# The MLP's second product of an adaLN block, by output features instead of by tokens

## The chip, the cores and the metric

The kernel runs on one core of one Trainium2 chip. The metric is the device time of the program in microseconds (us): the median of 3 runs before is 785.61 us (784.95 to 787.28). TensorE (PE) multiplies, VectorE (DVE) and ScalarE (ACT) work on vectors, GpSimd (POOL) does small things and issues some transfers, and SyncE (SP) issues most of the transfers. Matmul results go to PSUM, which the kernel uses as eight banks of 128 partitions x 512 numbers of 4 bytes.

## The reference

One transformer block, 2048 tokens of 640 features, with a modulation that is drawn from a single vector c. The second half is what matters here:

```python
mod = (_silu(c) @ w_mod).reshape(c.shape[0], 6, 1, -1)
sa, ca, ga, sb, cb, gb = (mod[:, i] for i in range(6))
h = _layernorm(x, axis=-1) * (1 + ca) + sa
x = x + ga * _A_ref(h, A_wqkv, A_w_phi, A_wo)      # linear attention, 32 heads of 20
h = _layernorm(x, axis=-1) * (1 + cb) + sb
# _B_ref: F = 1728
h = jnp.einsum("bsd,df->bsf", h, w1) + b1
r = jnp.where(h > 0, h, 0)
h = r * r
out = jnp.einsum("bsf,fd->bsd", h, w2) + b2
x = x + gb * out
```

## The kernel before

Every large product is computed in three terms: each operand is split into a rounded high half and the rest (`three`: high x high, high x low, low x high). ScalarE makes the high half by a copy into the rounded type, VectorE the low half by a subtraction (`lo`, line 80, so all of them show as L80). `mm` (line 70) issues the matmuls, so all of them show as L70; the tiles' names tell them apart.

**Stages.** First the projections and the state of the attention (to about 265 us), then the attention's output for the first 1024 tokens, then the MLP in four groups `g` of 512 tokens (`GW`): groups 0 and 1, then `attend` (attention's output for the last 1024 tokens, pairs of token tiles `j` = 4 to 7), then groups 2 and 3. In the last two stages the order of PE, DVE and ACT is written out by hand (`manual_schedule`): the program order of the Python code is the order on each of these engines. SP and POOL are ordered by a planner. The first 265 us are mostly ordered by that planner too.

**One group.** The hidden layer is cut into 14 chunks `f` of 128 features (the last has 64). Step f of `group` issues the first product of chunk f (`up_mm`: 15 matmuls of 512 columns, weights standing, tokens moving), its ReLU, square and split (`up_relu`, `up_out`), and the second product of chunk f - 2 (`down`, LAG = 2). `down` has the tokens stand (128 x 128 of the squared hidden layer, tile r2t) and the weights w move, 640 columns in cuts of 384 and 256: 4 token tiles x 2 cuts x 3 terms = 24 matmuls a chunk, 16 in the last. The sums stay in PSUM for the whole group: four banks of tag pj (tile acc) and two of tag m (tile acr). `up_mm` is left with one bank of tag tp (odd f) and the third of tag m (even f).

**The end of a group.** For each token tile `finish` multiplies the sums by the gate gb (`gb_b`, spread over all partitions) and adds the residual, to which `add_b2` added b2 x gb before. `residual` loads the residual x1 as four tiles of 128 tokens, one store per tile writes the output. In the last group the gate is multiplied into W2 instead (`round2`: multiply on DVE, high half on ACT, low half on DVE).

**Weights.** W1 stays for the most part; four chunks of W1 and all of W2 go through a ring of six slots, loaded some chunks ahead (`ring_loads`). For W2 the raw chunk is read and rounded again (`round2`, L1477), the low half is read from a copy in DRAM.

**Around attention.** `late_blocks`/`late_turn` load and turn blocks of the attention's features (32 x 32 transposes on DVE, L948), `num` multiplies them with the state on PE, `num_hi` and `num_lo` split the result on ACT and DVE, `do_wo` multiplies with wo and adds the residual. `ln2`, `back`, `turn`, `affine`, `split2` make the next groups' inputs H2. Buffers are rows of tags s1 to s4, x, k, q0, q1 and w (`BUFS`); an instruction that writes a new tile waits until the slot's last user is done.

## Time and profile before

| | us |
|---|---|
| median of 3 runs | 785.61 (784.95 to 787.28) |
| the profiled execution | 786.04 |
| its span | 784.3 |
| first matmul of group 0, from the span's start | 348.0 |
| group 1's first up matmul | 445.2 |
| attention for the last 1024 tokens, its first matmul | 535.5 |
| group 2's first matmul | 589.1 |
| last matmul | 779.8 |

The granted clock of TensorE is 0.999 over the span. Busy shares over the span: PE 99%, DVE 71%, ACT 51%, POOL 10%. By stage, VectorE is busy 68.8 of the 97 us from 348 to 445, 76.9 of the 91 us to 536, 43.3 of the 61 us to 597, 37.1 of the 87 us to 684, and 54.6 of the last 100 us; the DMA engines' share in the same stages is 0.84, 0.78, 0.69, 0.58 and 0.31.

How to read the rows: times are us from the span's start. A row of a group of instructions has line, engine, operation, out<-in, shape of the output (partitions x elements), count, then busy time in us, mean ns of one, then the idle time of the engine before them and who ended it. A timeline row has start, length, engine, line, operation, shape, count, and in brackets the wait before it. A row of the windows has the stretch, its length, then busy time (and count) of PE, its weight loads, DVE, ACT and POOL, the granted clock, the share of the DMA engines and GB/s. Rows of transfers have KB of one and the median us from issue to landing; rows of one tile give min/median/max in ns.

### The profile page before, as it was taken

Reading aid. Unit: us, or ns where it says so; the run is one execution under the profiler, and the core shown is the slowest. Engines: PE = TensorE matmul, PEld = TensorE weight load, DVE = VectorE, ACT = ScalarE, POOL = GpSimd, SP = SyncE. Lnnn points to the kernel's source line nnn. Section 1 sums busy time; section 2 is a strip of 40 time slices with the busy share of each in tenths; the row PEclk is TensorE's granted clock in tenths of the full one; section 3 lists DMA queues with packets and bytes.
Section 4 is the critical chain, followed back from the end, with each engine's and each line's share of the span. In section 5 each row is a group of like instructions: output and inputs, shape, how many; then the busy total and the mean of one; then the engine's idle time right before and its main releaser. Section 6 shows DMA issues by size and latency. Waiting matters only on the chain.

```text
span 784.3 us, 13311 instructions
## 1 busy us (share of the span) xinstructions
PE 775.4 (99%) x5163; PEld 716.2 (91%) x5163; DVE 553.4 (71%) x917; ACT 402.7 (51%) x789; POOL 78.8 (10%) x181
## 2 busy tenths in 40 slices
PE   9999999999999999999999999999999999999997
PEld 8899999999998988898999989998999999989997
DVE  4499899999766488664869799957945353575544
ACT  4667576546744344655957355432365544433221
POOL 3002020001100022201323000100010000000000
PEclk9999999999999999999999999999999999999999
DMA  9613248234121254476799757996679855145121
GB/s 339 259 36 132 101 164 290 91 129 153 55 85 34 84 191 137 163 223 234 254 313 336 236 182 250 262 364 189 189 238 353 280 162 158 51 151 201 34 84 68
DMA packets 76437, 142.31 MB, mean 181 GB/s; under 512 B 12718, under 2 KB 37422, under 8 KB 76374
## 3 DMA queue, kind: packets, MB, share of 16 engines
q1 hardware_dynamic: 69094, 117.41, 45.7%
q0 software_dynamic: 4096, 16.78, 5.7%
q10 hardware_dynamic: 3184, 7.27, 2.6%
q8 instruction: 40, 0.66, 0.3%
q14 instruction: 23, 0.19, 0.1%
HBM read 98.40 MB, written 42.93 MB: 180 GB/s over the span
## 4 chain that ended last, share of the span: by engine, by line
PE 82%; DVE 7%; DMA 4%; ACT 3%; POOL 2%; issue 1%; SPq 0%; ACTq 0%; DVEq 0%; POOLq 0%
PE up L70 22%; PE acc L70 14%; PE acr L70 9%; PE pv L70 9%; PE pk L70 9%; PE pq L70 8%; PE pwo L70 4%; PE kvp L416 3%; DVE dn L814 2%; DVE scr L812 1%; DMA rw<-in_w 1%; PE ta L326 1%; DVE ezb L833 1%; DMA xb<-in_x 1%; DMA w<-w2d 1%
## 5 line engine op out<-in xcount | busy, mean ns | idle before, releaser
L70 PE MATMUL up<-h,w 128*128 128x512 f32 (+1 forms) x910 | 198.2, 371 | 1.1 <-ACT r L1375 0.8
L70 PEld LDWEIGHTS up<-h,w 128*128 128x128 f32 x910 | 155.8, 188 | 29.1 <-DVE h L80 1.2
L70 PE MATMUL acc<-w,r2t 128*128 128x384 f32 x656 | 150.8, 336 | 0.0
L70 PE MATMUL acr<-w,r2t 128*128 128x256 f32 x656 | 112.9, 279 | 0.0
L70 PEld LDWEIGHTS acc<-w,r2t 128*128 128x128 f32 x656 | 107.5, 188 | 4.2 <-DVE w L80 0.2
L70 PEld LDWEIGHTS acr<-w,r2t 128*128 128x128 f32 x656 | 105.6, 188 | 0.0
L70 PE MATMUL pwo<-wo,ot 128*128 128x320 f32 (+1 forms) x512 | 79.5, 313 | 0.1
L70 PE MATMUL pk<-wk,hT 128*128 128x320 f32 x480 | 79.1, 313 | 0.1
L70 PE MATMUL pv<-wv,hT 128*128 128x360 f32 (+1 forms) x480 | 78.3, 312 | 0.0
L70 PE MATMUL pq<-wq,hT 128*128 128x320 f32 x480 | 76.7, 314 | 0.5 <-ACT k L392 0.4
L70 PEld LDWEIGHTS pwo<-wo,ot 128*128 128x128 f32 (+1 forms) x512 | 75.8, 188 | 1.1 <-DVE xm L1044 0.4
L70 PEld LDWEIGHTS pk<-wk,hT 128*128 128x128 f32 x480 | 71.5, 188 | 2.5 <-issue 0.9
L70 PEld LDWEIGHTS pv<-wv,hT 128*128 128x128 f32 x480 | 72.4, 188 | 0.4
L70 PEld LDWEIGHTS pq<-wq,hT 128*128 128x128 f32 x480 | 70.6, 188 | 2.1 <-ACT k L392 1.3
L1375 ACT ACTIVATE r<-up,b_t 128x512 f32<-128x512 f32 x52 | 35.0, 680 | 67.6 <-PE up L70 59.6
L80 DVE TENSOR_TENSOR r2t<-r,r2t 128x512 fp32r<-128x512 f32 (+1 forms) x56 | 38.3, 685 | 32.9 <-ACT r2t L1387 30.1
L1386 DVE TENSOR_TENSOR r<-r 128x512 f32<-128x512 f32 x26 | 17.9, 690 | 47.0 <-ACT r L1375 47.0
L80 DVE TENSOR_TENSOR w<-rw,w 128x640 fp32r<-128x640 f32 (+2 forms) x42 | 33.3, 814 | 23.6 <-ACT w L1074 12.1
L1387 ACT ACTIVATE r2t<-r 128x512 fp32r<-128x512 f32 x52 | 32.9, 632 | 22.4 <-DVE r L1386 21.6
L1477 ACT ACTIVATE w<-rw 128x640 fp32r<-128x640 f32 x42 | 30.6, 730 | 26.4 <-DVE rw L1476 24.1
L339 ACT ACTIVATE hfa<-ta,cols_a 128x256 f32<-128x256 f32 x30 | 17.0, 565 | 27.0 <-PE ta L326 25.8
L1074 ACT ACTIVATE w<-rw 128x640 fp32r<-128x640 f32 x28 | 19.4, 727 | 16.6 <-DMA rw<-in_w 7.5
(241 smaller groups left out, 1078.9 us busy)
## 6 DMA issues: line engine op xcount, KB each, us to landing
rw<-in_w SPq DMA_DIRECT2D x65, 320.0 KB, 4.5
w<-w2d SPq DMA_DIRECT2D x28, 320.0 KB, 6.0
w<-w1d SPq DMA_DIRECT2D x12, 640.0 KB, 6.6
esp<-eq SPq DMA_DIRECT2D x11, 640.0 KB, 3.2
wm<-in_w_mod SPq DMA_DIRECT2D x20, 320.0 KB, 3.6
xb<-in_x SPq DMA_DIRECT2D x8, 640.0 KB, 4.4
el<-esp SPq DMA_DIRECT2D x8, 640.0 KB, 4.0
xx<-in_x SPq DMA_DIRECT2D x16, 320.0 KB, 3.7
```

Of the source, the lines that this page charges most:

```text
L70: nc.tensor.matmul(o, a, b, start=first and i == 0, stop=last and i == len(terms) - 1, skip_group_check=skip,)
L80: (eng or nc.vector).tensor_tensor(out_lo, full, hi.bitcast(F32), op=ALU.subtract)
L326: nc.tensor.transpose(p[:, i * P : (i + 1) * P], xn[:, i, d * P : (d + 1) * P], ident)
L339: nc.scalar.activation(hf, p[:, :256], AF.Identity, bias=cols[:, d : d + 1], scale=cols[:, 5 + d : 6 + d])
L416: nc.tensor.matmul(kvp[64 * c : 64 * c + 64, g // 4, a : a + 2 * n].rearrange("p (s n) -> p s n", s=2), v[:, u], e[:, :, o : o + n], start ...
L812: nc.vector.tensor_tensor(z, flat(ET[t]), flat(zb), op=ALU.mult)
L814: nc.vector.tensor_reduce(dn.rearrange("p s h -> p (s h)"), heads(z), axis=AX.X, op=ALU.add)
L1074: nc.scalar.activation(w[:, 0], RAW[k, f], AF.Copy)
L1375: nc.scalar.activation(r, UP[f], AF.Relu, bias=b1_t[:, f : f + 1])
L1386: nc.vector.tensor_tensor(r, r, r, op=ALU.mult)
L1387: nc.scalar.activation(t[:, 0], r, AF.Copy)
L1477: nc.scalar.activation(w[:, 0], raw, AF.Copy)
```

## The change

The second product is turned round. The weights of chunk f stand, 128 of the 640 output features at a time (five output chunks k), and all 512 tokens move: 15 matmuls of 512 columns a chunk, 10 for the last. The sums are then features x tokens, in five banks (four pj, one m), and `up_mm` has three banks in rotation. Since an output feature is now a partition, gate and b2 x gate are columns of one number per partition: ScalarE applies both while it evicts (`gated`, scale and bias). VectorE transposes the result in 32 x 32 blocks and adds the residual, which is loaded in the layout that these blocks have (`residual`, `finish`), and the output is stored from there in rows of 640 bytes (`store`). The output features are permuted in the weights w2, b2 and part 5 of w_mod, as before in parts 3 and 4.

The order at the ends of groups changes with it. After groups 0 and 2, three chunks are evicted and finished at the group's end, chunks 3 and 4 in steps 0 and 1 of the next group. After group 1 all five are evicted between the last matmuls, three are finished there and two in `attend` at j = 5, and the store follows there. The turning of block 5 moves from group 1's end into its steps 12 and 13. In the last group the first product of the last chunk is put ahead, the second products of chunks 10 to 13 run output chunk by output chunk, the last two output chunks in halves of 256 tokens; W2 isn't multiplied by the gate any more, and its low half is read as in the other groups. The stores of x1 for j = 4, 5 are issued on ACT, xx5 has another buffer, and tag s3 has five rows instead of three.

```diff
-BUFS = {"w": 21, "x": 2, "k": 2, "q0": 1, "q1": 1, "s1": 3, "s2": 2, "s3": 3, "s4": 5}
+BUFS = {"w": 21, "x": 2, "k": 2, "q0": 1, "q1": 1, "s1": 3, "s2": 2, "s3": 5, "s4": 5}
...
-    gb_b = const.tile([P, D], F32, name="gb_b")
-    bb = const.tile([P, D], F32, name="bb")
+    gate = const.tile([P, NC], F32, name="gate")
+    b2g = const.tile([P, NC], F32, name="b2g")
...
-    X1 = [dram.tile([P, 2, D], F32, name=f"x1_{j}") for j in range(NT // 2)]
+    X1 = [dram.tile([2 * P, D], F32, name=f"x1_{j}") for j in range(NT // 2)]
...
-        yield from mod_rows(5, gb_b)
-        t = row("s1", "b2s")
-        nc.sync.dma_start(t, bass.AP(tensor=b2.tensor, offset=b2.offset, ap=[[0, P], [1, D]]))
-        nc.vector.tensor_tensor(bb, t, gb_b, op=ALU.mult)
+        yield from mod_cols(5, gate)
+        nc.sync.dma_start(b2g, b2)
...
-                nc.sync.dma_start(X1[j], XM[j])
+                (nc.sync if j < FIRST else nc.scalar).dma_start(X1[j].rearrange("(i p) d -> p i d", p=P), XM[j])
...
-            XX[j] = [row("s4" if j == 5 else "s2" if j < 4 else "s1", f"xx{j}_{i}") for i in range(2)]
+            XX[j] = [row("s2" if j < 6 else "s1", f"xx{j}_{i}") for i in range(2)]
...
-    def behind_sp():
-        return tc.issue_after([i for i in nc.cur_bb.bb.instructions if i.engine == ET_.SP][-1])
+    def behind(engine):
+        return tc.issue_after([i for i in nc.cur_bb.bb.instructions if i.engine == engine][-1])
...
-            UP[f] = tp(f"up{g}_{f}") if f % 2 and f != extra else bank(f"up{g}_{f}")
+            UP[f] = tp(f"up{g}_{f}") if f % 3 == 1 else bank(f"up{g}_{f}")
...
-    ACC, XR = {}, {}
-    CUT = 384
-
-    def residual(g):
-        with behind_sp():
-            for i in range(4):
-                t = XR[g, i] = row("s4", f"xr2_{g}_{i}")
-                nc.sync.dma_start(t, X1[2 * g + i // 2][:, i % 2])
-
-    def add_b2(g):
-        for i in range(4):
-            nc.vector.tensor_tensor(XR[g, i], XR[g, i], bb, op=ALU.add)
-
-    def down(g, f, tiles=range(4)):
+    ACC, XR, YT = {}, {}, {}
+
+    def residual(g, r):
+        if r == 0:
+            XR[g] = []
+        rows = g + 1 < NGR
+        t = row("s4", f"xr{g}_{r}") if rows else flat(tok2("x", f"xr{g}_{r}"))
+        XR[g].append(t)
+        n = P if rows else 2 * P
+        j, at = divmod(n * r, 2 * P)
+        src = X1[2 * g + j][at : at + n].rearrange("(b i) f -> i b f", i=32)
+        with behind(ET_.PE):
+            for a in range(4):
+                nc.sync.dma_start(t[32 * a : 32 * a + 32].rearrange("p (b f) -> p b f", f=160), src[:, :, 160 * a : 160 * a + 160])
+
+    def down(g, f, ks=range(NC), cols=None):
         t, n, w = R2[g, f], FS[f], W2[f]
-        for i in tiles:
-            if f == 0:
-                if i == 0:
-                    big = pj(f"acc{g}_0") + pj(f"acc{g}_1")
-                    rest = [bank(f"acr{g}_{h}") for h in range(2)]
-                    for h in range(4):
-                        ACC[h] = (big[h][:, :CUT], rest[h % 2][:, 256 * (h // 2) : 256 * (h // 2) + 256])
-            s = slice(i * P, (i + 1) * P)
-            for h, cs_ in enumerate((slice(0, CUT), slice(CUT, D))):
-                if n == P:
-                    terms = three(t[:, 0, s], t[:, 1, s], w[:, 0, cs_], w[:, 1, cs_])
-                else:
-                    terms = [(t[:, 0, s], w[:, 0, cs_]), (t[:, 0, s], w[:, 1, cs_])]
-                mm(ACC[i][h], terms, first=(f == 0 and (h == 0 or i < 2)), last=(f == NF - 1), skip=(h == 1))
-
-    def finish(g, i):
-        y, more = XR[g, i], g + 1 < NGR
-        z = row("s3", f"z{g}_{i}") if more else None
-        for h, cs_ in enumerate((slice(0, CUT), slice(CUT, D))):
-            src = ACC[i][h]
-            if more:
-                nc.vector.tensor_tensor(z[:, cs_], src, gb_b[:, cs_], op=ALU.mult)
-                src = z[:, cs_]
-            nc.vector.tensor_tensor(y[:, cs_], src, y[:, cs_], op=ALU.add)
-        t = 4 * g + i
-        nc.sync.dma_start(out[t * P : (t + 1) * P], y)
+        c = cols or slice(0, GW)
+        for k in ks:
+            if f == 0 and k == 0:
+                ACC.update(enumerate(pj(f"acc{g}_0") + pj(f"acc{g}_1") + [bank(f"acc{g}_4")]))
+            hi, low = (w[:, s, k * P : (k + 1) * P] for s in range(2))
+            terms = [(hi, t[:, 0, c]), (hi, t[:, 1, c]), (low, t[:, 0, c])] if n == P else [(hi, t[:, 0, c]), (low, t[:, 0, c])]
+            mm(ACC[k][:, c], terms, first=(f == 0), last=(f == NF - 1), skip=(g == NGR - 1 and k > 2))
+
+    def gated(g, k, cols=slice(0, GW)):
+        if cols.start == 0:
+            YT[k] = row("s3", f"yt{g}_{k}")
+        nc.scalar.activation(YT[k][:, cols], ACC[k][:, cols], AF.Identity, bias=b2g[:, k : k + 1], scale=gate[:, k : k + 1])
+
+    def finish(g, k, cols=slice(0, GW)):
+        n = GW // len(XR[g])
+        y = row("s3", f"y{g}_{k}")
+        nc.vector.transpose(*(t[:, cols].rearrange("p (b e) -> p b e", e=32) for t in (y, YT[k])))
+        for r in range(cols.start // n, cols.stop // n):
+            to = XR[g][r].rearrange("p (b f) -> p b f", f=160)[:, :, 32 * k : 32 * k + 32]
+            nc.vector.tensor_tensor(to, y[:, n * r : n * r + n].rearrange("p (b e) -> p b e", e=32), to, op=ALU.add)
+            if k == NC - 1 and g + 1 != FIRST // 2:
+                store(g, r, n)
+
+    def store(g, r, n):
+        at = GW * g + n * r
+        dst = out[at : at + n].rearrange("(b i) f -> i b f", i=32)
+        src = XR[g][r].rearrange("p (b f) -> p b f", f=160)
+        for a in range(4):
+            q = nc.scalar if a % 2 and r and g + 1 == NGR else nc.sync
+            q.dma_start(dst[:, :, 160 * a : 160 * a + 160], src[32 * a : 32 * a + 32])
...
-                if gg < NGR - 1:
-                    nc.sync.dma_start(w[:, 1].bitcast(F32), WD[k][i])
+                nc.sync.dma_start(w[:, 1].bitcast(F32), WD[k][i])
...
-    def round2(g, f):
+    def round2(f):
         if 0 <= f < NF:
-            n, w, raw = FS[f], W2[f], RAW[f]
-            if g == NGR - 1:
-                nc.vector.tensor_tensor(raw, raw, gb_b, op=ALU.mult)
-            nc.scalar.activation(w[:, 0], raw, AF.Copy)
-            if g == NGR - 1:
-                if n < P:
-                    nc.gpsimd.memset(w[n:, 1].bitcast(F32), 0.0)
-                lo(w[:n, 1], raw[:n], w[:n, 0])
+            nc.scalar.activation(W2[f][:, 0], RAW[f], AF.Copy)
 
     LAG = 2
+    BY_CHUNK = NF - 4
...
+                for k in (3, 4):
+                    finish(FIRST // 2 - 1, k)
...
+                with behind(ET_.SP):
+                    for r in range(4):
+                        store(FIRST // 2 - 1, r, P)
...
+        owed = g not in (0, FIRST // 2)
...
-            else:
+            elif more or f < NF - 1:
...
-            if f == (6 if g else 11):
-                residual(g)
-            if f == 9 and g:
-                add_b2(g)
+            for r in range(4 if more else 2):
+                if f == min(r + (6 if g else 11), NF - 1):
+                    residual(g, r)
...
+                if f > 11:
+                    late_turn(5, ("w", "w") if f == 12 else None, LAST[5], (range(5), range(5, 11))[f - 12])
...
+            if not more and f == NF - 2:
+                up_mm(g, NF - 1)
+            if not more and f == NF - 1:
+                down(g, BY_CHUNK - 1)
...
+            if owed and f < 2:
+                gated(g - 1, f + 3)
+                finish(g - 1, f + 3)
...
-            if f >= LAG:
+            if f >= LAG and (more or f - LAG < BY_CHUNK - 1):
...
-            down(g, NF - 1)
-        if more and not nxt:
+            for k in range(NC):
+                down(g, NF - 1, (k,))
+                if k < 3:
+                    gated(g, k)
+            for k in range(3):
+                finish(g, k)
+            return
+        if more:
             late_wo(range(3, NG))
             load_x1(4)
-        if g == 0:
-            add_b2(g)
-        for i in range(4):
-            for f in range(NF - LAG, NF) if not nxt else ():
-                down(g, f, (i,))
-            finish(g, i)
-            if i == 0 and more and not nxt:
+        full, halves = slice(0, GW), (slice(0, 256), slice(256, GW))
+        ends = [(k, full) for k in range(NC if more else 3)] + [(k, c) for c in halves for k in (3, 4) if not more]
+        for k, c in ends:
+            for f in range(NF - LAG if more else BY_CHUNK, NF):
+                down(g, f, (k,), c)
+            gated(g, k, c)
+            if not more or k < 3:
+                finish(g, k, c)
+            if k == 0 and more:
                 R2T.clear()
-                num(FIRST, [bank("numa4"), tp("numb4"), psA.tile([P, 512], F32, tag="pj", name="numc4", bufs=4)])
+                num(FIRST, [bank("numa4"), tp("numb4"), bank("numc4")])
                 num_hi(FIRST)
                 num_lo(FIRST)
-            if i in (1, 2) and more and not nxt:
-                late_turn(5, ("w", "w") if i == 1 else None, LAST[5], (range(5), range(5, 11))[i - 1])
...
-        for part in (3, 4):
+        for part in (3, 4, 5):
...
-        "w2": B_w2,
-        "b2": B_b2,
+        "w2": B_w2.reshape(F, 4, NC, 32).transpose(0, 2, 1, 3).reshape(F, D),
+        "b2": B_b2.reshape(4, NC, 32).transpose(1, 0, 2).reshape(NC, P).T,
```

More of the change, by code (lines that the diff above doesn't have):

```diff
@@ L476, in side @@
         nc.vector.tensor_scalar(cols_b[:, 5:10], cols_b[:, 5:10], 1.0, None, op0=ALU.add)
-        yield from mod_rows(5, gb_b)
-        t = row("s1", "b2s")
-        nc.sync.dma_start(t, bass.AP(tensor=b2.tensor, offset=b2.offset, ap=[[0, P], [1, D]]))
-        nc.vector.tensor_tensor(bb, t, gb_b, op=ALU.mult)
+        yield from mod_cols(5, gate)
+        nc.sync.dma_start(b2g, b2)
+        nc.vector.tensor_tensor(b2g, b2g, gate, op=ALU.mult)
         nc.sync.dma_start(b1_t, b1)
@@ L1137, in add_x @@
             nc.vector.tensor_tensor(XM[j][:, i], XM[j][:, i], XX[j][i], op=ALU.add)
-        nc.sync.dma_start(X1[j], XM[j])
+        nc.sync.dma_start(X1[j].rearrange("(i p) d -> p i d", p=P), XM[j])
     def ln2(j):
@@ L1347, with up_mm @@
     UP = {}
-    def up_mm(g, f, half=None, ds=range(NC), extra=None):
+    def up_mm(g, f, half=None, ds=range(NC)):
         if half is None or half == 0 and 0 in ds:
-            UP[f] = tp(f"up{g}_{f}") if f % 2 and f != extra else bank(f"up{g}_{f}")
+            UP[f] = tp(f"up{g}_{f}") if f % 3 == 1 else bank(f"up{g}_{f}")
         s = slice(0, GW) if half is None else slice(256 * half, 256 * half + 256)
@@ L1362, in up_start @@
         for f in range(n):
-            up_mm(g, f, 0, extra=3)
+            up_mm(g, f, 0)
         for d in range(NC):
@@ L1527, in attend @@
                 late_turn(7, ("w", "w"), LAST[7], range(11))
+                with behind(ET_.SP):
+                    for r in range(4):
+                        store(FIRST // 2 - 1, r, P)
             if j == 6:
@@ L1618, in group @@
                 up_out(g, 3)
+            if owed and f < 2:
+                gated(g - 1, f + 3)
+                finish(g - 1, f + 3)
             if g and (more or f == 0):
-                round2(g, f)
+                round2(f)
             late_exp()
```

3 lines of the change are left out of this document (1 added, 2 removed).

## The prediction

> **What bounds the kernel now.** I read the page's totals and chain first, then the groups of the matmuls, then who made PE wait.
>
> ```profile
> span 784.3 us, 13311 instructions
> ...
> PE 775.4 (99%) x5163; PEld 716.2 (91%) x5163; DVE 553.4 (71%) x917; ACT 402.7 (51%) x789; POOL 78.8 (10%) x181
> ...
> PE 82%; DVE 7%; DMA 4%; ACT 3%; POOL 2%; issue 1%; SPq 0%; ACTq 0%; DVEq 0%; POOLq 0%
> ...
> L70 PE MATMUL up<-h,w 128*128 128x512 f32 (+1 forms) x910 | 198.2, 371 | 1.1 <-ACT r L1375 0.8
> ...
> L70 PE MATMUL acc<-w,r2t 128*128 128x384 f32 x656 | 150.8, 336 | 0.0
> L70 PE MATMUL acr<-w,r2t 128*128 128x256 f32 x656 | 112.9, 279 | 0.0
> ```
>
> PE is busy 99% of the span and is 82% of the chain. The product to be rebuilt is acc and acr, 656 matmuls each, 263.7 us busy in all; up has nearly as many columns and only 198.2 us. It is tempting to read this as 402 ns for 640 columns before (230 + 172) against 218 ns for 512 after. But busy times of pipelined matmuls overlap and end where the trace models them; what counts is when the next one starts. The timeline of PE in group 2 gives that:
>
> ```profile
> 618.06 3.60 PE L70 MATMUL up<-h,w 128*128 128x512 f32 x15
> 621.50 0.68 PE L70 MATMUL acc<-w,r2t 128*128 128x384 f32 x3
> 622.02 0.51 PE L70 MATMUL acr<-w,r2t 128*128 128x256 f32 x3
> 622.36 0.68 PE L70 MATMUL acc<-w,r2t 128*128 128x384 f32 x3
> ...
> 624.94 3.60 PE L70 MATMUL up<-h,w 128*128 128x512 f32 x15
> ...
> 666.62 3.60 PE L70 MATMUL up<-h,w 128*128 128x512 f32 x15
> ```
>
> Fifteen up matmuls of 512 columns run from 618.06 to 621.50: 3.44 us, 229 ns each. From 618.06 to 666.62 are seven steps of one chunk f, 6.937 us each, so the old second product takes 6.937 - 3.44 = 3.497 us a chunk for 12 x 640 = 7680 columns. The new one has 15 x 512 = 7680 columns too. Columns per us are what PE sells, and the change sells the same number. And PE hardly ever waits; of all its waits this is the longest inside the MLP:
>
> ```profile
> PE up L70 <- ACT r L1375: 0.8, 1, 0.8
> ```
>
> So the MLP is a stream of columns without holes; a cheaper VectorE or ScalarE is worth nothing there by itself. What can move the time is the price per column, that one hole, the seams between groups, and the tail.
>
> **The stream.** I price a new chunk at up's 3.44 us, the same shape from the same kind of operands: 0.057 us saved on each of 52 full chunks, and 0.04 on each of 4 short ones (10 matmuls of 229 ns for 8 pairs of 3.497/12 = 291 ns). Together -3.1 us, and I take -2.9 because in the first steps shown the old chunk already ran at 3.44 (621.50 to 624.94), which the seven-step mean only partly holds. Bounds: 0 if the old pairs lose time to something that the new form meets as well, -5 if every new chunk undercuts up a little. The last group runs chunks 3 and 4 of outputs in halves of 256 columns, 44 short matmuls for 22 long ones: by 0.34 us for three of 256 in the rows above (622.02 to 622.36), 44 x 113 is no more than 22 x 229: 0.
>
> [...]
>
> **The hole.** The accumulators take five PSUM banks instead of six, so up has three instead of two.
>
> ```profile
> 368.10 0.74 ACT L1074 ACTIVATE w<-rw 128x640 fp32r<-128x640 f32 x1 [5.90 <-DMA rw<-in_w]
> 370.48 0.67 ACT L1375 ACTIVATE r<-up,b_t 128x512 f32<-128x512 f32 x1
> 371.20 3.72 PE L70 MATMUL up<-h,w 128*128 128x512 f32 x15 [0.79 <-ACT r L1375]
> ```
>
> In group 0 up(4) waits 0.79 us for relu(2) to empty its bank, because ScalarE stood 5.90 us behind a weight load. In the new rotation up(4) takes the bank of up(1), long empty. What is late next is down(2), one up product (3.44 us) further on; its operand follows the relu by about 2 us. Saved: -0.8 us, bounds 0 and -0.8.
>
> **The seams 0 to 1 and 2 to 3.** Gate and bias move to ScalarE's eviction, three chunks at the group's end and two owed to steps 0 and 1 of the next group; VectorE then turns and adds. Each eviction waits for PE's last matmul of its chunk; behind it on ScalarE stands the next relu, due a whole up product (3.44 us) later. Cover: the next group's down starts after three up products, 10.3 us, and reaches output chunk 4 last, 12 x 229 ns = 2.7 us later. In group 1 VectorE has no slack:
>
> ```profile
> 441.00:455.00 14.00, 14.00 (x74) 12.26 (x74) 13.73 (x26) 5.77 (x10) 0.00 (x0) 1.00 0.49 175
> 510.00:531.00 21.00, 21.00 (x120) 19.16 (x119) 10.75 (x23) 8.08 (x13) 1.24 (x3) 1.00 0.98 366
> ...
> 700.00:760.00 60.00, 60.00 (x338) 54.56 (x337) 31.26 (x43) 19.82 (x30) 0.00 (x0) 1.00 0.37 122
> ```
>
> It is busy 13.73 of 14 us at the seam. Per group it loses three passes over 4 x 640 columns (gate, add, b2: 7680) and gains five turns and five adds of 512 (5120 in 25 instructions): about equal at the seam, less at step 9 where b2 was added. I take 0; if the cover is gone, each us that VectorE is later than PE's need is one us lost. The residual now comes as 16 pieces of 640 B rows instead of 4, and the stores too: some 24 more issues a group on SP. Loads on SP run several chunks ahead, so I take 0.
>
> **The seam into attention.** Two edits cut opposite ways. The turning of block 5 (11 transposes) moves ahead into steps 12 and 13 of group 1, where the row above shows VectorE busy only 10.75 of 21 us. And two finishes move into the middle of attention, ahead of the split and the turning of block 7:
>
> ```profile
> 553.56 5.24 DVE L948 STREAM_TRANSPOSE et<-se 128x256 f32<-128x256 f32 x10
> ...
> 559.12 1.69 DVE L1044 TENSOR_TENSOR xm<-pwo,xx 128x320 f32<-128x320 f32 x4
> 561.62 0.69 DVE L80 TENSOR_TENSOR ot<-numa,ot 128x512 fp32r<-128x512 f32 x1 [0.80 <-ACT ot L1002]
> ...
> 564.23 5.24 DVE L948 STREAM_TRANSPOSE et<-se 128x256 f32<-128x256 f32 x10
> ...
> 569.83 0.88 DVE L1044 TENSOR_TENSOR xm<-pwo,xx 128x320 f32<-128x320 f32 x2
> ```
>
> A turn of 256 columns costs 0.505 us start to start here (11 from 553.56 to 559.12). A finish is one turn of 512, about 1.0 us, and four adds of 128 columns, between 0.17 (40 columns) and 0.36 (200):
>
> ```profile
> L885 DVE TENSOR_TENSOR late_z<-late_e,dn 128x200 f32<-128x200 f32 x30 | 8.8, 362 | 0.2
> ...
> L894 DVE TENSOR_TENSOR etl<-late_e,dn 128x40 f32<-128x40 f32 x10 | 1.3, 170 | 0.0
> ```
>
> I take 0.27, so 2.1 us a finish and 4.2 for two. The wait of 0.80 us at 561.62 takes up part of that, so VectorE is 3.4 us late from there on. Who waits: PE, for the split of block 6, and from 572.16 for the turned block 7:
>
> ```profile
> 562.48 9.75 PE L70 MATMUL pwo<-wo,ot 128*128 128x320 f32 x64
> ...
> 572.16 1.08 PE L70 MATMUL numa<-et,kvd2b 128*64 128x256 f32 x8
> ```
>
> Block 6 begins halfway through the 64, at about 567.3; the split (561.62 to 564.23 now) would come in parts from 565.7 to 567.6, the first read first. Block 7's turns would be done between 568.1 and 573.2, and the last is read after 574. Both just fit: 0, with +1.5 as the bound.
>
> **The last group.** W2 is no longer multiplied by the gate and split on VectorE; the low halves are read, 14 reads of 320 KB more. They come chunks ahead of PE, and the DMA engines carried 122 GB/s there (the last window above) against 366 before attention: 0. The tail is what ends the kernel:
>
> ```profile
> 779.79 0.39 PE L70 MATMUL acr<-w,r2t 128*128 128x256 f32 x2
> 779.99 0.56 DVE L1434 TENSOR_TENSOR xr<-acc,xr 128x384 f32<-128x384 f32 x1 [0.57 <-PE acc L70]
> 780.47 0.41 DVE L1434 TENSOR_TENSOR xr<-acr,xr 128x256 f32<-128x256 f32 x1
> ```
>
> ```profile
> L948 DVE STREAM_TRANSPOSE et<-se 128x256 f32<-128x256 f32 x40 | 21.2, 673 | 0.0
> ...
> L339 ACT ACTIVATE hfa<-ta,cols_a 128x256 f32<-128x256 f32 x30 | 17.0, 565 | 27.0 <-PE ta L326 25.8 <-DVE hT L80 1.2
> ```
>
> ```profile
> sb<-xn SPq DMA_DIRECT2D x32, 160.0 KB, 3.4
> ...
> out<-xr SPq DMA_DIRECT2D x16, 320.0 KB, 2.5
> ```
>
> ```profile
> L1161 SPq DMA_DIRECT2D sb<-xn x32: 551/606/4057, 328.5 to 658.7; - x32
> ```
>
> ```profile
> L1436 SPq DMA_DIRECT2D out<-xr x16: 332/340/1141, 447.6 to 780.9; - x16
> ```
>
> Before: the last matmul ends near 780.18, two adds follow to 780.88, one store is issued (0.34 us) and lands in about 2.5; 784.3 is 3.4 us behind the adds. After: an eviction of 256 columns from PSUM with scale and bias (0.57), a turn (0.67), an add (0.41), with hand-overs 1.7 us instead of 0.7: +1.0. Then four stores of 160 KB in 640 B rows, two on SP and two on ScalarE's queue. The sb loads of that form take 0.61 us to issue instead of 0.34 and 3.4 to land; the second on each queue starts one issue later, and SP has four stores of the first half just before: +0.9. Tail +1.9, bounds +1.0 and +3.0. VectorE keeps up before that: a half costs it about 1.1 us against PE's 11 x 113 = 1.25.
>
> **Small edits.** Part 5 of the modulation as columns (five transposes and two reductions for two matmuls and two evictions), the small b2 load, the row layout of x1, its two stores on ScalarE's queue (in program order behind a matmul and an add that ScalarE's next work waits for anyway), the other buffers of xx5, two more s3 rows: 0 each. The s3 rows can also reorder the automatically ordered first 265 us; I keep ±1.5 us for it.
>
> **Sum**, against the profiled execution's own 786.04 us (span 784.3): -2.9 - 0.8 + 1.9 = -1.8, so 784.2. The median of the runs before, 785.61, is 0.43 us below that execution, so I give 783.8.
>
> **Rivals.** (a) The forecast, 783.8, own range 782 to 786: 0.52, of which 0.15 lies below 783.25.
> (b) The tail costs its lower bound (+1.0), and the row buffers free ScalarE in attention so that group 2 starts without the short waits on its inputs (0.5 us): 782.4 or less. For it: three rows of s3 are few where two are held across a step. Against: group 2's second half of inputs comes by a chain that the added finishes delay. 0.22.
> (c) Slower: the turning of block 5 is put ahead of group 1's last products on VectorE and needs two w slots there. If they are free only when the last up product releases its inputs (near 530.6), the second six turns (3.1 us) run ahead of the last chunk's four VectorE and ScalarE steps:
>
> ```profile
> 522.58 2.61 SPq L1470 DMA_DIRECT2D wo<-wod  x3
> ```
>
> ```profile
> 526.92 0.69 DVE L80 TENSOR_TENSOR r2t<-r,r2t 128x512 fp32r<-128x512 f32 x1 [6.27 <-ACT r2t L1387]
> 531.39 0.68 DVE L1391 TENSOR_TENSOR r<-up,r 64x512 f32<-64x512 f32 x1 [3.78 <-ACT r L1390]
> ```
>
> That work starts at 531.4 now and PE, by its steps of 6.9 us, takes the result near 535; it would start at 537 and PE would stand about 5 us: 788.8. It decides as soon as a slot comes later than about 528. Against: three loads into w slots were issued at 522.58, so slots were free by then. 0.13.
> (d) The squeezed attention costs its bound: 785.3. 0.11.
> (e) The price per instruction is large and 492 fewer pay it: if the busy times were the true prices, 820 x 218 ns = 179 us for 263.7, -85 us and 701. Against: 3.44 and 3.497 us a chunk for the same columns. 0.02. [...]
>
> **How the numbers follow.** About 0.3% (2.36 us) is what a measurement of this kernel can tell from no change: faster is below 783.25, slower above 787.97. Faster: 0.15 + 0.22 + 0.02 = 0.39; slower: (c) and 0.02 of (d), 0.15; same 0.46. The range 781.0 to 788.0 leaves out (c), (e) and the far end of (b), under 0.2.
>
> **What would show it.** Chunk steps of 6.88 us in the timeline of PE instead of 6.94; no wait near 371; the last matmul near 776.5; from it to the end 6.0 us instead of 4.2. The prediction is wrong if PE has waits at a seam (VectorE's rows near 527 to 575 tell which), or if the matmuls of the new form are spaced other than 229 ns.

## The result, and the profile after

The changed kernel takes 798.33 us (median of 6 runs, 793.5 to 800.53), the kernel before 786.3 us: a ratio of 1.0145, 95% interval 1.0114 to 1.0177. It is slower by 12 us where 1.8 us less were forecast. Its profiled execution took 796.88 us with a span of 795.1, so 10.8 us of span are to be found. These are the first lines of its page, and from the chain the shares by engine:

```profile
span 795.1 us, 12493 instructions
...
PE 778.1 (98%) x4694; PEld 683.5 (86%) x4694; DVE 527.1 (66%) x911; ACT 414.9 (52%) x809; POOL 77.6 (10%) x180
...
PE 74%; DVE 10%; DMA 5%; ACT 5%; issue 2%; SPq 2%; POOL 1%; ACTq 0%; DVEq 0%; POOLq 0%
```

DMA and SP's issues are 7% of a chain where they were 4%. The sums of busy time don't say where; marks along TensorE's work do. Each row of this table is the start of a matmul in the timeline of PE; the last column is a version of the changed kernel that comes further down.

| start of, us | before | after | late | fix3 |
|---|---|---|---|---|
| group 0, first up | 348.0 | 348.4 | +0.4 | 348.5 |
| group 1, first up | 445.2 | 446.9 | +1.7 | 445.0 |
| attention, first num | 535.5 | 536.6 | +1.1 | 534.8 |
| group 2, first up | 589.1 | 590.5 | +1.4 | 588.6 |
| group 2, first acc | 607.6 | 613.3 | +5.7 | 606.2 |
| group 2, up of chunk 5 | 618.1 | 626.4 | +8.3 | 616.6 |
| group 3, first up | 685.1 | 693.1 | +8.0 | 683.3 |
| the last matmul | 779.9 | 787.5 | +7.5 | 777.6 |
| end of the span | 784.3 | 795.1 | +10.8 | 785.3 |

The last matmul before starts at 779.9; 779.8 in the first table is the start of its row of two. So the loss has four places: group 0 (1.3 us), the start of group 2 (4.3), its chunk 2 (2.6), and the end (3.2). Groups 1 to 3 give back 0.3 to 0.6 us each elsewhere. Attention, where the prediction looked for a loss, runs as before. Whom PE waited for from 345 us on (waited for: us, times, longest):

```profile
PE acc L70 <- ACT w L1478: 2.4, 1, 2.4
PE acc L70 <- DVE r2t L80: 2.1, 2, 1.9
PE up L70 <- ACT h L1195: 0.8, 2, 0.6
```

In all 0.8 us before, 5.3 now. Two of the three stand in the timeline of PE:

```profile
418.20 3.48 PE L70 MATMUL acc<-r2t,w 128*128 128x512 f32 x14 [1.88 <-DVE r2t L80]
...
622.81 3.72 PE L70 MATMUL acc<-r2t,w 128*128 128x512 f32 x15 [2.39 <-ACT w L1478]
```

**The wait at 416 to 418.** VectorE's timeline shows why the split r2t was late: it is queued behind the turning of block 2, which waited for its input. The row by itself is the same place before the change.

```profile
413.39 2.25 DVE L1170 STREAM_TRANSPOSE fa_q<-sb 128x256 f32<-128x256 f32 x4 [5.93 <-DMA sb<-xn]
415.46 0.70 DVE L1171 STREAM_TRANSPOSE fa_q<-sb 128x256 f32<-128x256 f32 x1
415.98 1.56 DVE L80 TENSOR_TENSOR w<-rw,w 128x640 fp32r<-128x640 f32 x2
417.46 0.68 DVE L80 TENSOR_TENSOR r2t<-r,r2t 128x512 fp32r<-128x512 f32 x1
```

```profile
411.62 2.23 DVE L1171 STREAM_TRANSPOSE fa_q<-sb 128x256 f32<-128x256 f32 x4 [4.14 <-DMA sb<-xn]
```

Before, VectorE stood 4.14 us there, until 411.62, and PE had work enough to see nothing of it.

**Group 2's start and its chunk 2** hang together in the chain of waits (start, length, what), and both go through SP:

```profile
571.04 0.44 SPq L1441
...
573.51 5.84 DMA out<-xr
579.39 0.60 SPq L1160
580.04 0.71 SPq L1160
580.80 6.29 DMA sb<-xn
587.12 0.73 DVE fa_q L1170 x2
...
616.98 0.36 SPq L1460
617.45 4.55 DMA rw<-in_w
622.02 0.74 ACT w L1478
```

L1441 is the output's store: the store of group 1, which now stands in the middle of attention, is what the inputs of group 2 (sb, L1160) come behind. SP's timeline shows it in full, after and then before:

```profile
565.07 11.16 SPq L1441 DMA_DIRECT2D out<-xr  x16
...
578.79 2.66 SPq L1160 DMA_DIRECT2D sb<-xn  x4
...
591.95 2.50 SPq L1160 DMA_DIRECT2D sb<-xn  x4
...
601.94 2.60 SPq L1408 DMA_DIRECT2D xr<-x  x4
...
614.34 2.53 SPq L1408 DMA_DIRECT2D xr<-x  x4
...
617.45 0.85 SPq L1459 DMA_DIRECT2D rw<-in_w  x2
```

```profile
576.56 2.58 SPq L1161 DMA_DIRECT2D sb<-xn  x4
...
586.42 2.82 SPq L1161 DMA_DIRECT2D sb<-xn  x4
...
602.12 0.32 SPq L1403 DMA_DIRECT2D xr<-x  x1
...
604.64 2.33 SPq L1454 DMA_DIRECT2D rw<-in_w  x2
```

Sixteen pieces of output take SP 11.2 us. Block 4's input, asked for behind them, is issued 2.2 us later than before (578.79, 576.56) and also lands more slowly: it is turned 5.7 us after its last piece was issued (587.12), before 3.9 (583.00). In the chain, one of its pieces is issued (579.39) only when a piece of the store, under way for 5.84 us, has landed; both go over one of the eight semaphores that SP's transfers use in the trace. Block 5's input is asked for 5.5 us later than before. Then sixteen pieces of residual (xr) stand between SP and the raw chunk 2 of W2 (rw): the first of them is issued at 601.94, rw at 617.45, though ScalarE had freed its row at 610.3 (its rounding of chunk 0 runs from 609.59, 0.72 us). Before there were four reads, and rw was issued when the row came free.

**The end.** The last rows of the timeline; the last matmul starts at 787.45:

```profile
786.71 3.64 SPq L1441 DMA_DIRECT2D out<-xr  x6
...
787.77 0.56 ACT L1423 ACTIVATE yt<-acc,b2g,gate 128x256 f32<-128x256 f32 x1 [0.73 <-PE acc L70]
788.36 0.45 DVE L1428 STREAM_TRANSPOSE y<-yt 128x256 f32<-128x256 f32 x1 [0.39 <-ACT yt L1423]
788.84 0.43 DVE L1431 TENSOR_TENSOR xr<-y,xr 128x256 f32<-128x256 f32 x1
789.30 1.12 ACTq L1441 DMA_DIRECT2D out<-xr  x2
```

Evict, turn and add end 1.5 us behind the last matmul's end (787.73), where 1.7 was priced. From there to the end of the span it is 5.8 us; it was 3.4.

**Half clock.** PE's records show a fifth cost that no row of waits names. Between 593.9 and 597.4 the granted clock was 0.5; a stretch like it stands behind the wait at 416 to 418 in other runs, xr2_behind among them. The windows before, in and behind such a stretch, from the run xr2_behind below (length, then busy us and count of PE, PEld, DVE, ACT, POOL, the granted clock, DMA share, GB/s):

```profile
414.70:418.10 3.40, 1.57 (x7) 1.01 (x6) 3.40 (x6) 0.00 (x0) 1.08 (x2) 0.99 0.88 184
418.10:421.50 3.40, 3.40 (x9) 2.62 (x9) 3.33 (x8) 2.80 (x5) 1.62 (x3) 0.51 1.03 375
421.50:424.90 3.40, 3.40 (x16) 2.77 (x16) 3.40 (x13) 1.65 (x3) 1.31 (x3) 1.00 1.05 398
```

In the first, one matmul starts 2.2 us after the one before it; the next stretch, of the same length, runs at half clock (0.51): 9 matmuls of 512 columns where the next has 16. By half of 3.4 us that is an estimated 1.7 us lost on top of the wait. Whether it comes differs from run to run, and with it part of the spread of the times: 793.5 us with a mean clock of 0.998, 800.53 with 0.992.

### The profile page after: what moved, and what is told of

It reads as the page before. It is cut to its first block, busy times and chain, and to the rows that moved or that the text cites. A ratio compares the mean times of both kernels' runs of the same rounds, so it can differ in the third digit from the quotient of the medians.

```text
span 795.1 us, 12493 instructions
## 1 busy us (share of the span) xinstructions
PE 778.1 (98%) x4694; PEld 683.5 (86%) x4694; DVE 527.1 (66%) x911; ACT 414.9 (52%) x809; POOL 77.6 (10%) x180
## 4 chain that ended last, share of the span: by engine, by line
PE 74%; DVE 10%; DMA 5%; ACT 5%; issue 2%; SPq 2%; POOL 1%; ACTq 0%; DVEq 0%; POOLq 0%
PE acc L70 20%; PE up L70 18%; PE pv L70 9%; PE pk L70 8%; PE pq L70 8%; PE kvp L416 3%; PE pwo L70 2%; DMA sb<-xn 2%; DMA rw<-in_w 2%; DVE dn L813 2%; DVE scr L811 1%; DVE et L947 1%; PE ta L326 1%; DVE ezb L832 1%; SPq L1160 1%
## 5 line engine op out<-in xcount | busy, mean ns | idle before, releaser
L70 PE MATMUL up<-h,w 128*128 128x512 f32 (+1 forms) x910 | 201.2, 374 | 1.3 <-ACT h L1195 0.8
L70 PE MATMUL acc<-r2t,w 128*128 128x512 f32 (+1 forms) x842 | 197.6, 388 | 4.5 <-ACT w L1478 2.4
L70 PEld LDWEIGHTS up<-h,w 128*128 128x128 f32 x910 | 161.0, 190 | 34.3 <-DVE h L80 2.2
L70 PEld LDWEIGHTS acc<-r2t,w 128*128 128x128 f32 x842 | 155.3, 188 | 39.3 <-DVE r2t L80 3.1
L1170 DVE STREAM_TRANSPOSE fa_q<-sb 128x256 f32<-128x256 f32 x32 | 18.0, 690 | 19.2 <-DMA sb<-xn 19.2
L80 DVE TENSOR_TENSOR w<-rw,w 128x640 fp32r<-128x640 f32 (+2 forms) x28 | 21.7, 809 | 11.9 <-ACT w L1073 11.8
L407 DVE TENSOR_REDUCE sk<-ek 128x64 f32<-128x1280 f32 x16 | 23.7, 1480 | 3.9 <-ACT ek L403 3.9
```

The costliest lines, as they stand in the source:

```text
L70: nc.tensor.matmul(o, a, b, start=first and i == 0, stop=last and i == len(terms) - 1, skip_group_check=skip,)
L80: (eng or nc.vector).tensor_tensor(out_lo, full, hi.bitcast(F32), op=ALU.subtract)
L407: nc.vector.tensor_reduce(s, heads(flat(e)), axis=AX.X, op=ALU.add)
L1170: nc.vector.transpose(FA[k][:, at : at + 256].rearrange("p (t b) -> p b t", b=8), src[:, 2 * k + d])
```

## The experiments

Theory R (rows): four times as many DMAs with rows a quarter as long fill SP's queue and the DMA engines. Theory O (order): the new reads and stores stand in the wrong place of the queues. The kernels of the table below issue the same 4694 matmuls in one order, so each matmul can be set against the same one of the changed kernel. How late the profiled execution of each is against that of the changed kernel, in us, at the times of the latter (minus is earlier), the us from the last matmul's start to the end, and the median of its runs:

| run | 410 | 430 | 480 | 590 | 600 | 620 | 640 | last matmul | to the end | median |
|---|---|---|---|---|---|---|---|---|---|---|
| after | 0 | 0 | 0 | 0 | 0 | 0 | 0 | 0 | 7.6 | 798.33 |
| res_rows | +0.5 | +2.5 | +2.5 | +2.5 | +2.8 | +1.3 | -1.4 | -1.4 | 7.8 | 795.15 |
| out_rows | +0.3 | +0.2 | +2.1 | +2.9 | -1.0 | -2.4 | -4.0 | -4.0 | 6.1 | 790.03 |
| both_rows | -0.1 | +1.4 | +3.7 | +12.7 | +8.8 | +7.4 | +4.7 | +4.7 | 6.3 | 796.64 |
| xr2_behind | -0.6 | +1.0 | +1.0 | +1.0 | +1.6 | +1.6 | -1.0 | -1.1 | 7.6 | 795.65 |
| turn_later | -0.6 | -2.8 | -2.8 | -2.8 | -1.7 | -3.1 | -1.8 | -1.8 | 7.9 | 794.69 |
| store_early | -0.1 | +1.6 | +1.6 | +1.6 | -2.3 | -3.7 | -4.5 | -4.5 | 7.7 | 791.88 |
| tail3 | +1.0 | +2.5 | +2.5 | +2.5 | +3.3 | +1.9 | +3.1 | +3.1 | 9.1 | 799.41 |
| fix3 | +0.3 | -1.8 | -1.8 | -1.8 | -5.7 | -7.1 | -9.8 | -9.9 | 7.7 | 787.37 |

A jump between two columns is what happened there. The rise of 1.5 to 2.0 us between 410 and 430 in five of them is the half clock behind the wait at 416, which the profiled execution of the changed kernel escaped; that execution had its half clock at 594 instead. Between 590 and 600 a half clock begins in the five profiles that keep group 1's store as it is (after, res_rows, xr2_behind, turn_later, tail3) and in none of the four that write it in whole rows or move it, so some 1.7 us of the falls of those four between 590 and 620 is that stretch.

### Whole rows: res_rows, out_rows, both_rows

```diff
             for a in range(4):
-                nc.sync.dma_start(t[32 * a : 32 * a + 32].rearrange("p (b f) -> p b f", f=160), src[:, :, 160 * a : 160 * a + 160])
+            nc.sync.dma_start(t.rearrange("p (i d) -> p i d", d=D), X1[2 * g + j][at : at + n].rearrange("(i p) d -> p i d", p=P))
...
-        for a in range(4):
-            q = nc.scalar if a % 2 and r and g + 1 == NGR else nc.sync
-            q.dma_start(dst[:, :, 160 * a : 160 * a + 160], src[32 * a : 32 * a + 32])
+        nc.sync.dma_start(out[at : at + n].rearrange("(i p) d -> p i d", p=P), XR[g][r].rearrange("p (i d) -> p i d", d=D))
```

The first part alone is res_rows, the second out_rows, both together both_rows. Whole rows don't fit the layout of the turned blocks: these kernels do the same work, but residual or outputs belong to the wrong tokens, so they are no versions to use.

> The residual of each 128 tokens (256 in the last group) is read in one DMA of whole 2560-B rows in place of four of 640-B rows; it is then added to other tokens' outputs. Theory R (pieces: four times as many DMAs with rows a quarter as long fill SP's queue and the DMA engines): the 2.39 us stall of TensorE at 622 and most of the 1.88 us one at 418 go, so about 794.2. Theory O (place: it is where these reads stand in the order that hurts, whatever their rows): both stalls stay, 798. The start of group 2 (4.3 us late against the kernel before) and the tail stay in both.

> The output of each 128 tokens (256 in the last group) is written in one DMA of whole 2560-B rows in place of four of 640-B rows, so the rows of out are permuted. Theory R: group 1's store no longer holds SP's queue for 11.2 us nor the DMA engines, so the inputs of group 2 come about 4 us earlier, and the end after the last matmul falls from 7.4 us to about 6: 792.8. Theory O (the store stands ahead of the inputs' loads, and 1.3 MB is 1.3 MB): group 2's start stays late, only the tail gains, 797.

> Reads of the residual and stores of the output both in whole 2560-B rows, so the output is permuted and the residual belongs to other tokens; all of the arithmetic stays. Theory R: every stall named so far is gone and what is left is the new stream, about 786.5, within 1.5 us of the kernel before. Theory O: 796.5. If the new product itself, its finishes or its seams cost time, it stays above 789 with no DMA wait behind it.

out_rows: 790.03 us, ratio to the kernel before 1.0059 (1.0033 to 1.0085). Its store is four issues in 2.3 us:

```profile
567.76 2.30 SPq L1439 DMA_DIRECT2D out<-xr  x4
...
576.73 2.60 SPq L1160 DMA_DIRECT2D sb<-xn  x4
...
587.53 2.87 SPq L1160 DMA_DIRECT2D sb<-xn  x4
```

Group 2 gains 6.9 us from 590 to 640 and the end 1.5: R, in group 2 and at the end, with the store at the same place. res_rows (795.15 us; 1.0116, 1.0094 to 1.0139) gains 2.7 us at chunk 2 and nothing at 416: R there, and R is wrong for the wait at 416, which every whole-row run still has. both_rows missed by 10 us (796.64; 1.0137, 1.0111 to 1.0164): it gains 8.0 us in group 2, as the two together should, but loses before it. Whom PE waited for in it:

```profile
PE acc L70 <- DVE r2t L80: 4.3, 4, 2.0
PE pwo L70 <- DMA wo<-wod: 3.6, 2, 2.4
PE acc L70 <- ACT w L1475: 1.1, 1, 1.1
```

Fewer pieces made the planner order SP's queue anew, and the weights wo of attention landed late (and PE ran at half clock for two stretches behind that; the mean clock of this execution is 0.993). The planner's order of SP is a term of its own in each of these runs. out_rows also loses 1.9 us between 430 and 480, in a wait for a split r2t of VectorE at 480; why that split is late was not followed up.

### The place of the reads: xr2_behind

```diff
+                ISSUED[gg, i] = [x for x in nc.cur_bb.bb.instructions if x.engine == ET_.SP][-1]
...
-        with behind(ET_.PE):
+        with tc.issue_after(ISSUED[2, 5]) if g == 2 else behind(ET_.PE):
```

> Only the order on SP's queue is changed: group 2's 16 reads of the residual are issued behind the load of that group's raw chunk 5 and no longer ahead of that of chunk 2. If the queue's place makes chunk 2 late (Theory O, and the queue's half of R), the 2.39 us stall at 622 goes and the time is 795.8. If the DMA engines are simply full there, the chunk lands as late as now and the time stays at 798.

```profile
612.00 2.33 SPq L1459 DMA_DIRECT2D rw<-in_w  x2
```

795.65 us (1.0139, 1.0101 to 1.0177), and the wait at 622 is gone: -2.6 us between 620 and 640. With the same pieces in the same rows it is the queue's place that made chunk 2 late; theory O and the queue's half of R say the same here.

### Three edits of order: turn_later, store_early, fix3

turn_later, and below it store_early; fix3 is both and xr2_behind.

```diff
-                if f == 8:
+                if f == 8 and g:
                     fa_new()
                     turn(a)
...
             if g == FIRST // 2 and f == 2:
                 up_out(g, 3)
+            if g == 0 and f == 8:
+                fa_new()
+                turn(a)
```

```diff
-                for k in (3, 4):
-                    finish(FIRST // 2 - 1, k)
                 la = ln2(a)
...
-                with behind(ET_.SP):
-                    for r in range(4):
-                        store(FIRST // 2 - 1, r, P)
...
-            if not more or k < 3:
-                finish(g, k, c)
+            finish(g, k, c)
...
-            if k == NC - 1 and g + 1 != FIRST // 2:
+            if k == NC - 1:
                 store(g, r, n)
```

> Only in group 0's step 8 the turning of block 2 moves on VectorE from ahead of the activations' split to behind it. Theory H (the hole filled at 371 brings TensorE to the turning 0.9 us earlier while the turning's input lands when the DMA engines let it, so the wait came back at 416): the stall of 2.1 to 2.4 us there goes, and with it the stretch of half clock that follows it in three of the four profiles shown since (1.7 us each): 794.5 to 796. If the second product waits for something else there, the split only changes its place in the queue and the time stays at 798.

> Group 1's finishes 3 and 4 and its output store (still 16 pieces of 640-B rows) are issued at the group's end, before attention, where the DMA engines stood idle from 545 to 557 in the profile after. Theory O, place: the store is out of the way of group 2's inputs, which come 4 us earlier, and the finishes cost at most their 3.2 us of VectorE if attention's first turning waits for them: 794 (up to 797). If 640-B rows hurt wherever they stand, attention's own loads are late instead and the time is 798 or more.

> The turning of group 0's step 8 behind the split, group 1's finishes and store before attention, and group 2's residual reads behind its raw chunk 5, all three; the computation is that of the changed kernel. If the three are separate waits their gains add: 2.6 (reads' place, as measured) plus 4 plus 2 to 4, so 788 to 790. If they share one cause, full DMA engines, the sum is much less, 793 or more.

turn_later: 794.69 us (1.0096, 1.0066 to 1.0126). VectorE splits first and then waits for the block, and PE's wait at 416 is gone:

```profile
413.19 2.25 DVE L1170 STREAM_TRANSPOSE fa_q<-sb 128x256 f32<-128x256 f32 x4 [1.65 <-DMA sb<-xn]
```

The input lands about when it did in the changed kernel (413.39); only PE's next operand no longer stands behind it. store_early: 791.88 us (1.0067, 1.0034 to 1.0099).

```profile
548.93 8.81 SPq L1441 DMA_DIRECT2D out<-xr  x16
...
574.40 3.71 SPq L1160 DMA_DIRECT2D sb<-xn  x4
...
585.86 2.50 SPq L1160 DMA_DIRECT2D sb<-xn  x4
```

The store is the same sixteen pieces, in the stretch where the DMA engines stood idle (at most 11 GB/s in slices of 1.5 us from 546 to 556.5 in the changed kernel), and block 5's input is asked for at 585.86 and not 591.95. From 590 to 640 it gains 6.1 us, about what whole rows gain (6.9), and the two finishes before attention cost attention nothing. So for group 2's start O and R are two ways out of one collision: many pieces on SP just ahead of the inputs.

fix3: 787.37 us (1.0012, 0.9984 to 1.0039), 11 us below the changed kernel, a little more than expected. The gains add: from 345 us on its profile lists no wait of PE at all, and the last matmul starts 2.3 us earlier than before the change. What is left of the loss is the end, 7.7 us against 4.4.

### The hole: fix3_hole

```diff
-            UP[f] = tp(f"up{g}_{f}") if f % 3 == 1 else bank(f"up{g}_{f}")
+            UP[f] = tp(f"up{g}_{f}") if f % 2 and f != (3 if g == FIRST // 2 else -1) else bank(f"up{g}_{f}")
```

> fix3 with the accumulators of the first product alternating between two banks as in the kernel before, not three. If the 0.9 us hole at 371 and waits like it are worth what the prediction said, once nothing else stands in their way: 0.8 us slower than fix3, 788.2, with the gap back near 371. If group 0 is held by its transfers anyway, the same as fix3, 787.4.

787.15 us (1.0015, 1.0001 to 1.0028), no gap near 371, and the same distance from fix3, 0.4 us earlier, at every mark from 410 on. The even chunks still have two banks here, since the accumulators take one less, so this did not bring the hole back; it shows only that the new rule of rotation, given three banks, earns nothing. What the hole is worth is to be read elsewhere (below).

### The end: tail3, halves_all, cut384, split_cols

```diff
-            q = nc.scalar if a % 2 and r and g + 1 == NGR else nc.sync
+            q = (nc.sync, nc.scalar, nc.gpsimd, nc.scalar)[a] if r and g + 1 == NGR else nc.sync
```

> The last four pieces of output are issued on three queues (SP 1, ACT 2, POOL 1) in place of two each on SP and ACT. If the queues' issue times make the end long, it gains 0.5 us or more of the 5.8 us between the last add and the end: 797.6. If it is the transfer of 640-B rows itself, as the 1.5 us that whole rows gave at the end say, nothing: 798.3.

799.41 us (1.0144, 1.0086 to 1.0202), and the end grew to 9.1 us: a third queue, GpSimd's, is no help. halves_all and cut384 are fix3 with

```diff
-        full, halves = slice(0, GW), (slice(0, 256), slice(256, GW))
-        ends = [(k, full) for k in range(NC if more else 3)] + [(k, c) for c in halves for k in (3, 4) if not more]
+        full, halves = slice(0, GW), (slice(0, 256), slice(256, GW))
+        ends = [(k, full) for k in range(NC)] if more else [(k, c) for c in halves for k in range(NC)]
```

and 384 in place of 256 in cut384, which also loads the last group's residual as four tiles of 128 tokens.

> The three edits of fix3, and at the end of the last group all five chunks are cut in two halves of 256 tokens, all first halves ahead of all second ones, so the first half's store is issued about 6.5 us before the last add and no longer 2.6. If the end is long because two stores of 640-B rows run one after the other, it falls from 7.6 us to about 6.5 and the time is 786.3, that of the kernel before. If the last store alone sets it, the end stays at 7.5 and the time at 787.4.

> As halves_all, but cut at token 384, so the last store has 128 tokens (320 KB in all) and the last matmuls move 128 columns. If the store's bytes set the end, it falls by half of their transfer, 1 us or more, to about 6 us after the last matmul: 786. If 128 columns cost TensorE nearly as much as 256 (55 matmuls, 117 ns each as the halves take now), TensorE ends about 3 us later: 788.

halves_all: 788.53 us (1.0028, 1.0016 to 1.0039), the end 7.4: the earlier first store gives 0.2, so it is the last store that sets the end, and PE began the halves with a wait of 0.43 us for r2t. cut384: 788.95 us (1.0035, 1.0018 to 1.0051). The end falls to 5.9 us, as hoped, but PE pays it back. Its rows of 128 columns, and those of 256 in the changed kernel:

```profile
779.07 5.86 PE L70 MATMUL acc<-r2t,w 128*128 128x128 f32 x51
```

```profile
782.75 4.98 PE L70 MATMUL acc<-r2t,w 128*128 128x256 f32 x41
```

From start to start that is 112 ns for 128 columns against 118 for 256. So the bytes of the last store have to be cut in columns, not in tokens. split_cols is fix3 with

```diff
+            if not more and k == NC - 1 and c.start == 0:
+                store(g, 1, 256, slice(0, 96))
             finish(g, k, c)
...
-                store(g, r, n)
+                store(g, r, n, slice(96, 160) if r and g + 1 == NGR else slice(0, 160))
```

> fix3, and of the last 256 tokens the columns that chunks 0 to 2 make (96 of each 160) are stored as soon as TensorE is in the halves, so only 64 of each 160 are left for the last store: 256 KB in place of 640. If the transfer of the last store sets the end, the 7.6 us after the last matmul fall to about 6 and the time is 785.9, below the kernel before. If the issue of the pieces or a fixed time from issue to landing sets it (there are now twelve pieces in place of eight, and at most eight are under way), the end stays at 7.5 or grows: 787.4 or more.

786.05 us beside 786.03 for the kernel before, run with it: a ratio of 1.0001 (0.9992 to 1.001). The end is 6.4 us. It is the best version found; it takes back the whole loss and does not beat the kernel before.

### The input at 413: fetch_shift, warm24

```diff
+    for i in range(32):
+        nc.tensor.matmul(warm[:, :16], ones, ones[:, :16], start=True, stop=True)
```

```diff
-WARM = 10
+WARM = 24
```

> The changed kernel with 32 small matmuls more in the warming up at the start, whose product nobody reads; they shift the reading of TensorE's code, which in all nine profiles since the change falls at 409 to 410 with 1.0 us on one DMA engine, while block 2's input is read. From the first packet of that input to its turning it takes 7.2 to 7.6 us in all nine, 6.1 in the profile before, where no such fetch falls there. If the fetch is the cause, this run shows 6.1 to 6.4 with the fetch elsewhere, and a stall at 416 of about 1 us in place of 2.1; if not, 7.2 again.

> The changed kernel with 24 warming-up matmuls of full size at the start in place of 10, which nobody reads; TensorE starts its work some 6 us later, and the reading of its code falls about 7 us earlier against the work. If the fetch that falls into block 2's input in every profile since the change delays it, the time from that input's first packet to its turning falls from 7.2 to 7.6 us to at most 6.4. If not, it stays above 7.

The question is whether a fetch of instructions, taken here for TensorE's code, holds up block 2's input: 16 KB on the DMA queue q8, 1.08 us from 409.13 in the changed kernel. Neither run settled it. fetch_shift had a granted clock of 0.78 over its first 100 us, the changed kernel 1.00 (826.93 us in all, one run); its input took 6.7 us from first packet to turning, with no such fetch in between, which lies between the two expectations. warm24 (806.7 us, one run) moved the fetch by 3.8 us against the input, only to its first packet, and the input took 7.35 us. Why block 2's input lands 1.8 us later than before stays open.

## Why the prediction was wrong, point by point

**"Loads on SP run several chunks ahead, so I take 0"** is the step that failed, and it failed by most of the loss: 2.6 us at chunk 2 and, by the store, 4.3 at group 2's start. It priced some 24 more issues a group, for residual and stores, by where loads stand on average. At group 2's start they don't run ahead: the row for raw chunk 2 comes free at 610.3, 10 us before PE needs the chunk, load and rounding take 5.3 us, and the residual pieces in front of it hold SP until 617 (2.6 us, shown by xr2_behind).

**The seam into attention** was priced for VectorE only, at 0 with +1.5 as bound, and there it was right: attention took 53.9 us, before 53.6, and store_early shows that the two finishes cost nothing in either place. But the step moved the store too, and the store's sixteen issues on SP, ahead of the loads of group 2's inputs, were among those priced at 0. With the store elsewhere or in whole rows the stretch from 590 to 620 is 5.3 us shorter (store_early, out_rows and fix3 agree), of which 1.7 are the half clock; against the kernel before it is 4.3, since that one took 1.0 us longer there than fix3, by the table of marks.

**The hole**: the gap at 371 is gone, but the 0.8 us is not earned. Group 0 took 97.2 us before and 96.5 in fix3, about what the stream alone gives for its steps (0.6). The lead that fix3 has at 378 (0.6 us) is gone by 399.0, where the same step starts in both kernels; on the way a weight load waits 0.59 us for VectorE's split (395.67). ScalarE waits until 401.4 for a landing before and after the change, and block 2 is turned as its input lands, at 411.6 and 413.4: that transfers hold group 0 is argued from these waits. In the changed kernel PE met the turning of block 2. "What is late next" was asked for the next chunk and not for the stage. That the order on VectorE turned this into a wait is shown by turn_later (2.2 us, and up to 1.7 more by the half clock); that the input itself came 1.8 us later is seen and not explained.

**The stream** was right in kind and a little large. Steps after the change:

```profile
626.37 3.61 PE L70 MATMUL up<-h,w 128*128 128x512 f32 x15
...
681.50 2.49 PE L70 MATMUL up<-h,w 128*128 128x512 f32 x10
```

Eight steps in 55.13 us are 6.891 us a step, not 6.88; before 6.937. That is 0.046 us on 52 chunks, -2.4 us and not -2.9; in the marks of fix3 the four groups are together 2.1 us shorter, group 2 from its first acc on.

**The tail**: +1.9 was forecast and +3.2 measured (7.6 against 4.4). The chain of evict, turn and add was nearly right, 1.5 us for 1.7; the stores were mis-sized, 2.4 us more than before where +0.9 was forecast. Whole rows end at 6.1 us. The prediction took a piece's time from the sb loads; here the last four pieces of 640-B rows alone set the end, as halves_all shows (7.4 us with the first store earlier). The GB/s of the last rows' windows, 0.225 us a slice, before and after (776 to 785, 787 to 796):

```profile
GB/s 0 0 0 0 0 0 341 455 387 273 0 0 137 444 410 398 69 0 0 421 387 398 251 0 0 205 410 398 387 57 36 0 0 0 0 0 0 0 0 0
```

```profile
GB/s 0 0 60 196 182 188 182 179 188 131 168 302 324 273 213 142 205 287 296 296 287 256 248 253 245 236 211 196 83 0 0 0 0 0 0 0 0 0 0 0
```

About 410 GB/s with 2560-B rows while a store runs, mostly 180 to 320 with 640-B rows.

**The rivals.** (c) did not happen: the turning of block 5 in steps 12 and 13 held nobody up. (d) did not either. Of (b), the tail went the other way, but group 2 does start without its short waits in fix3 (1.0 us). Of (e), matmuls of the new form are spaced as priced, at 6.891 us a step. The case that did, stores and reads in pieces ahead of loads that are due, was not among them; the profile of before had the row for it (SP asks for the inputs of group 2 at 576.56 and 586.42, and VectorE turns them as they land, at 583.0 and 592.7).

**The sum** now, for fix3 against the kernel before: stream -2.4, hole 0, the start of group 0 and attention +0.8, group 2's start -1.0, end +3.2, together +0.6; its profiled span is 0.9 us longer and its median 1.1. The waits and the half clock behind them are the other 11 us of the changed kernel.

## What to carry to other kernels

When an edit moves a step, move its transfers in the account as well: count the pieces, find the queue they stand in, and look which load behind them is due next; an average share of the DMA engines (0.69 over the stage of attention before) said nothing about that place. A gain on the busiest engine in a stage that transfers seem to hold may not be earned (the 0.8 us of the hole here), and it can come back as a wait at the next thing they deliver (1.88 us at 418). In a stream of matmuls that hardly ever stops, a wait of about 2 us can cost nearly twice its length, when a stretch of half clock follows it (in xr2_behind 1.8 us of wait and an estimated 1.7 by the clock).

## What the runs showed of the hardware

**The half clock** came in stretches of 3.4 us: a granted clock of 0.50 from 593.93 to 597.35 in the changed kernel, 0.51 from 418.10 to 421.50 in xr2_behind. The one in xr2_behind stands behind a wait of 1.8 us. The changed kernel waited 1.88 us until 418.20 and 2.39 us until 622.81 with a clock of 1.00 in the 3.4 us behind each, and out_rows waited up to 1.8 us at a mean clock of 0.999, which leaves no room for such a stretch. So the length of the wait alone doesn't tell whether one follows, and what does was not shown.

**128 columns** cost TensorE almost as much as 256 in these runs: 112 ns (cut384) and 118 (the changed kernel) from start to start, and 229 for 512 (15 up matmuls in 3.44 us before the change).

**The turn of 32 x 32 blocks** was cheaper than priced: 0.71 us for 512 columns, and 0.45 for 256 in the last group, in the finishes, where both sides lie in order. The turns it was priced from take 0.68 for 256; they read in blocks and write with a stride of eight. That the layout makes the difference was not tried by itself. A finish took 1.6 us and not 2.1:

```profile
L947 DVE STREAM_TRANSPOSE et<-se 128x256 f32<-128x256 f32 x40 | 21.4, 680 | 0.7 <-PE acc L70 0.7
...
L1431 DVE TENSOR_TENSOR xr<-y,xr 128x128 f32<-128x128 f32 x60 | 13.5, 287 | 0.5
L1428 DVE STREAM_TRANSPOSE y<-yt 128x512 f32<-128x512 f32 x18 | 12.7, 708 | 9.1 <-ACT yt L1423 9.1
```
